# Half of the second group's first layer by twenty products, with its sums and a pair of halves put elsewhere in the order

## The chip, the cores and the metric
The kernel runs on one core of one Trainium2 chip. The metric is the device time of one execution in microseconds (us); smaller is better. The core has five engines with queues of their own: TensorE (PE, matmul), VectorE (DVE), ScalarE (ACT), GpSimd (POOL) and SyncE (SP, which here issues DMAs).

## What is computed
The reference is a recurrent attention followed by a two-layer network, all in float32:

```
for t in range(S):                     # S = 768, head_dim = 48, batch 4, 8 heads
    state = alpha[t] * state + k[t] (outer) v[t]
    y[t]  = q[t] @ state
x = y as (3072 tokens, 384)
h = x @ w_in                           # 384 x 2048
g = h * sigmoid(h)                     # silu
out = g @ w_out                        # 2048 x 384
```

The change concerns h = x @ w_in for a part of the tokens, and the order in which sums of weights, sums of tokens and sums of g are made.

## The kernel before, in words
**Tokens.** The 3072 tokens are 24 chunks of 128 (a chunk is 128 time steps of one of the four batches). Attention works chunk by chunk (`scores`, `products`, `quotient`, `values`, `states`, `flip`, `land`): DVE makes two scans, three transposes and some multiplies for each, PE the small matmuls, and `values` (L831) leaves the transposed output of two chunks in a tile `xt`. Four chunks make a group (six groups, `grp` 0 to 5); a group has two halves of two chunks, 256 tokens (`h` 0 and 1).

**First layer.** The 2048 columns of w_in are two pairs of quarters (`pair` 0 and 1), eight blocks of 128 columns each. There are two ways to make h for them:

- `enter_plain(grp, h, pair)` (L897) takes one half of the tokens and makes the eight column blocks in four pieces of two blocks, each block three matmuls of 128x256; ACT applies silu from PSUM to the tile of g (L909). Behind the fourth piece of groups above 0 stands `side_by_side` (L1016), which adds two cells of g on DVE (L1019).
- `enter(grp, pair)` (L917) takes both halves of the tokens at once and makes the same columns by 20 products instead of 24 (a 4x3 by 3x2 block product with fewer multiplications, listed in PRODUCTS, L349), each as two matmuls of 128x256. It needs 23 sums of blocks of w_in (SUMS_W, L335, made on DVE by `sums_w`, L589; some overwrite w_in, the others fill a tile `wx`), 11 sums of tokens (SUMS_X, L343, `sums_x`, L878, into `xc`), and puts the products together with 12 copies on ACT (L936, four of them into a tile `part` that has one buffer) and 14 additions on DVE (L944 and, for one, L587). It has seven steps, six of three products and one of two; the last step ends with `side_by_side` for both halves. Accumulators are three PSUM banks that take turns (`bank`, L894): a product that begins a new bank waits until the addition or copy that reads the old content is done.

Groups 0 and 1 use the plain way, groups 2 to 5 the other.

**Second layer.** `leave(grp, h)` (L1021) makes the output of a half by seven products of eight matmuls 128x192 each, with six subtractions of g on DVE (L1033), sums on DVE (L1074 to L1085) and stores (L1036 to L1045). It needs differences of w_out (`differences`, L600), which plain(1,0,0) makes.

**Order.** The list `pieces` (L1120 to L1136) holds generators of `enter_plain`, `enter`, `leave` and `sums_x` in their order; `fill` (L1166) runs as many of them after each slot of an attention step as the work done so far is behind an even pace, `phases` marking the places where the pace is set anew. Each step has four slots. For the stretch in question the order of the kernel before is:

- phase 0 ends with plain(1,0,0) and the seven steps of leave(0,0);
- phase 1: four pieces plain(1,1,0); then leave(0,1) by turns with four pieces plain(1,0,1) and four pieces plain(1,1,1);
- phase 2: sums_x(2); leave(1,0) by turns with enter(2,0); leave(1,1) by turns with enter(2,1); and so on for the later groups.

The sums of w_in are issued from `done()` (L1050), which each step of `leave` calls: leave(0,1) makes those of pair 0, leave(1,0) those of pair 1, four a step. `late` is filled, and with it `wx` allocated, by `settle()` (L1154) after slot 3 of step 7; by the pacing, leave(0,0) has then made three of its seven steps.

**Queues.** From `settle` on PE's instructions stay in program order (`in_order`, L381). Sums of weights and of tokens, the conversion of weights and the range checks on alpha and the weights (L685) keep their order among each other on DVE; the other DVE instructions are placed by the compiler's scheduler, and the order so found is fixed at compile time. The steps of the prediction refer to L909, L944, L1019, L1033 and the lines of attention (L696 transposes, L722 and L752 scans, L758 multiply).

Of the kernel before, what the change touches and what calls it, by code (L numbers as in the profile page):

```python
# [355 lines left out]
def quotients(  # L356
# [22 lines left out]
    late = {}  # L379
# [25 lines left out]
    GB = 4  # L405
# [183 lines left out]
    def sums_w(pair, upto):  # L589

        r = slice(2 * pair, 2 * pair + 2)
        while sums_done[pair] < min(upto, len(SUMS_W)):
            to, sa, a, sb, b = SUMS_W[sums_done[pair]]
            tc.keep_in_program_order(
                combine(block_w(to)[:, r], sa, block_w(a)[:, r], sb, block_w(b)[:, r]))
            sums_done[pair] += 1

    sums_done = [0] * (NQ // 2)

    def differences(i):  # L600

        if i < HF // 2:
            i = slice(2 * i, 2 * i + 2)
            tc.keep_in_program_order(
                dve.tensor_tensor(t1[:, i], b12[:, i], b11[:, i], ALU.subtract))
            dve.tensor_tensor(t2[:, i], b22[:, i], t1[:, i], ALU.subtract)
            dve.tensor_tensor(t4[:, i], b21[:, i], t2[:, i], ALU.subtract)
        else:
            i -= HF // 2
            side_by_side(0, i % 2, i // 2)  # L610
            i = slice(2 * i, 2 * i + 2)
            dve.tensor_tensor(b12[:, i], b22[:, i], b12[:, i], ALU.subtract)
# [265 lines left out]
    def sums_x(grp):  # L878
        xcs[grp] = late["xc"].tile([128, len(SUMS_X), TB], F32, name="xc")
        for to, sa, a, sb, b in SUMS_X:  # L880
            tc.keep_in_program_order(
                combine(block_x(grp, to), sa, block_x(grp, a), sb, block_x(grp, b)))
        yield
# [4 lines left out]
    def g_tiles(grp, pair):  # L888
        for h in range(2):
            gts[grp, h, pair] = gpool.tile([128, 4, 2, TB], F32, name="g")  # L890
# [6 lines left out]
    def enter_plain(grp, h, pair):  # L897

        if h == 0:
            g_tiles(grp, pair)  # L900
        xt = xts[2 * grp + h]
        for f in range(8 * pair, 8 * pair + 8, 2):
            ps = bank(f // 2 % 3).rearrange("p (e n) -> p e n", e=2)
            for e in range(2):
                for t in range(NKT):
                    pe.matmul(ps[:, e, :], lhsT=w_in[:, t, (f + e) * 128 : (f + e + 1) * 128],
                              rhs=xt[:, t, :], start=(t == 0), stop=(t == NKT - 1))
            q, i = divmod(f, 4)
            act.activation(gts[grp, h, pair][:, i : i + 2, q % 2, :], ps, AF.Silu)  # L909
            if grp == 1 and pair == h == 0:  # L910
                differences(f // 2)
                differences(4 + f // 2)
            if grp > 0 and f % 8 == 6:
                side_by_side(grp, h, pair)
            yield

    def enter(grp, pair):  # L917
        g_tiles(grp, pair)
        halves = [gts[grp, h, pair] for h in range(2)]

        s = [halves[o % 2][:, o // 2] for o in range(8)]
        todo = iter(PRODUCTS)

        def new(i):
            return bank(i).rearrange("p (e n) -> p e n", e=2)

        def add(ps, first=False):
            w, x = next(todo)
            for e in range(2):
                pe.matmul(ps[:, e], lhsT=block_w(w)[:, 2 * pair + e], rhs=block_x(grp, x),  # L930
                          start=(first and e == 0), stop=(e == 1), skip_group_check=True)

        def copy(ps, to=None):
            if to is None:
                to = late["part"].tile([128, 2, TB], F32, name="part")
            act.copy(to, ps)  # L936
            return to

        def silu(h, i):
            x = halves[h][:, i : i + 2]  # L940
            act.activation(x, x, AF.Silu)  # L941

        def tt(to, a, b, op=ALU.add):
            dve.tensor_tensor(to, a, b, op)  # L944

        a, b, c = [new(i) for i in range(3)]
        add(a, True)
        copy(a, s[6])
        add(b, True)
        copy(b, s[2])  # L950
        add(c, True)
        tt(s[6], s[6], copy(c), ALU.subtract)
        yield
        add(a)
        t = copy(a)
        add(b)
        copy(b, s[4])
        add(c)
        copy(c, s[7])
        tt(s[7], s[7], t, ALU.subtract)  # L960
        yield
        add(a)
        copy(a, s[5])
        add(b)
        copy(b, s[3])
        tt(s[5], s[5], s[3])
        add(c)
        copy(c, s[0])
        yield
        add(a)  # L970
        tt(s[4], a, s[4])
        b = new(1)
        add(b, True)
        add(b)
        copy(b, s[1])
        yield
        c = new(2)
        add(c, True)
        tt(s[2], s[2], copy(c), ALU.subtract)
        a = new(0)  # L980
        add(a, True)
        tt(s[6], a, s[6])
        silu(0, 2)
        add(b)
        tt(s[5], copy(b), s[5], ALU.subtract)
        yield
        add(c)
        tt(s[1], c, s[1])
        tt(s[3], s[1], s[3], ALU.subtract)
        a = new(0)  # L990
        add(a, True)
        tt(s[2], a, s[2])
        add(b)
        tt(s[7], b, s[7])
        silu(1, 2)
        yield
        add(c)
        combine(s[1], -1, s[1], -1, s[0])
        tt(s[0], c, s[0])
        silu(0, 0)  # L1000
        a = new(0)
        add(a, True)
        tt(s[3], a, s[3])
        silu(1, 0)
        turn.append(turn.pop(0))
        for h in range(2):
            side_by_side(grp, h, pair)
        yield
# [7 lines left out]
    def side_by_side(grp, h, pair):  # L1016

        x = cells(grp, h, pair, 1, 0)
        dve.tensor_tensor(x, x, cells(grp, h, pair, 1, 1), ALU.add)  # L1019

    def leave(grp, h):  # L1021
# [26 lines left out]
        steps = iter(range(7))  # L1048

        def done():  # L1050
            if 2 * grp + h in (1, 2):
                sums_w(2 * grp + h - 1, 4 * next(steps) + 4)

        def new(i):
            return out_bank(i, HO)
# [51 lines left out]
    def plain(grp, h, pair):  # L1107
        return (enter_plain(grp, h, pair), 12, 2 * (2 * grp + h) + 2)

    def group(grp):  # L1110
        return [[(enter(grp, pair), 12, GB * grp + GB)] * 7 for pair in range(2)]

    def output(grp):
        return [[(leave(grp, h), 12, GB * grp + GB)] * 7 for h in range(2)]
# [1 line left out]
    def both(x, y):  # L1116
        for i in range(max(len(x), len(y))):
            pieces.extend(x[i : i + 1] + y[i : i + 1])

    pieces = []  # L1120
# [3 lines left out]
    pieces += [plain(1, 0, 0)] * 4 + [(leave(0, 0), 12, GB)] * 7  # L1124
    phases = [len(pieces)]
    pieces += [plain(1, 1, 0)] * 4
    both([(leave(0, 1), 12, GB)] * 7, [plain(1, 0, 1)] * 4 + [plain(1, 1, 1)] * 4)
    phases.append(len(pieces))
    before = output(1)
    for grp in range(2, NG):  # L1130
# [10 lines left out]
    def go_on():  # L1141

        nonlocal done
        next(pieces[done][0], None)
        done += 1

    audits = audit()
    done, bridged = 0, 0
    STEPS = NT + 1
    SLOTS = 4  # L1150
# [148 lines left out]
```

## Time and profile before
| | us |
|---|---|
| median of 3 runs | 560.08 |
| lowest, highest run | 558.29, 560.13 |
| span of the profiled execution, first to last instruction | 558.1 |
| PE, DVE, ACT, POOL busy in it | 541.4, 445.1, 208.4, 75.9 |

Of the profiled execution only its span is known; what lies around it shows in the runs, the fastest of which is 0.2 us longer than the span. In the groups of the profile a name such as `ps_m<-xt,w_in` gives the output and inputs of an instruction; a float32 matmul of the source appears as two records. `ps_m` are the banks of the first layer, `ps_o` of the second, `ps_a` of attention. In a timeline the columns are start, duration, engine, line, operation and, in brackets, the idle time of the engine before it and what ended it.

### The profile page before, as it was taken

The page shows a single profiled execution, that of the slowest core. Times are in us where ns is not written, and L with a number is a line of the kernel's source. Part 1 is how long each engine was busy: PE and PEld are TensorE (multiplying, and loading weights), DVE is VectorE, ACT ScalarE, POOL GpSimd, SP SyncE. Part 2 cuts the span into 40 slices and gives each one's busy share as a digit, 9 for nine tenths or more (in the row PEclk, how much of TensorE's full clock was granted, in tenths as well). Part 3 has the DMA queues.
Part 4 walks back from the last instruction along what each step waited for, and adds up shares of the span by engine and source line. Part 5 has one row for each costly group of instructions (what it writes and reads, how often), then busy time and mean ns, then how long its engine had stood idle before and what let it go on. Part 6 is the DMA issues. An engine that isn't in the chain of part 4 may idle for free. (4 is left out here: it accounts for less than half of the span.)

```text
span 558.1 us, 12640 instructions
## 1 busy us (share of the span) xinstructions
PE 541.4 (97%) x5026; PEld 488.8 (88%) x5026; DVE 445.1 (80%) x801; ACT 208.4 (37%) x466; POOL 75.9 (14%) x146
## 2 busy tenths in 40 slices
PE   5999999999999999999999999999999999999996
PEld 3788887998899898899999999988998999998996
DVE  5887889974999799997998986998894775857531
ACT  3456643223333243353353353353263341432200
POOL 4100010221211211021021021021121000001000
PEclk9799999999999999999999999999999999999999
DMA  9999861164445525355445654717712122333101
GB/s 218 255 276 177 232 189 40 38 164 108 126 131 136 142 62 134 88 145 157 129 109 142 194 141 115 198 22 179 180 48 84 53 99 95 111 109 106 38 25 32
DMA packets 99220, 70.13 MB, mean 126 GB/s; under 512 B 56272, under 2 KB 88656, under 8 KB 99152
## 3 DMA queue, kind: packets, MB, share of 16 engines
q1 hardware_dynamic: 97232, 65.30, 44.6%
q0 software_dynamic: 1920, 3.93, 2.0%
q8 instruction: 41, 0.67, 0.5%
q14 instruction: 27, 0.22, 0.1%
HBM read 61.34 MB, written 7.86 MB: 124 GB/s over the span
## 5 line engine op out<-in xcount | busy, mean ns | idle before, releaser
L388 PE MATMUL ps_o<-w_out,g 128*128 128x192 f32 x768 | 134.7, 329 | 1.1 <-DVE o L1042 0.9
L388 PEld LDWEIGHTS ps_o<-w_out,g 128*128 128x128 f32 x768 | 125.4, 190 | 5.1 <-DVE o L1042 2.3
L388 PE MATMUL ps_m<-xt,w_in 128*128 128x256 f32 x480 | 113.6, 383 | 1.5 <-ACT xt L851 1.1
L388 PEld LDWEIGHTS ps_m<-xt,w_in 128*128 128x128 f32 x480 | 89.1, 190 | 14.4 <-ACT xt L851 1.6
L388 PE MATMUL ps_o<-wt,g 128*128 128x192 f32 x576 | 99.7, 326 | 0.0
L388 PEld LDWEIGHTS ps_o<-wt,g 128*128 128x128 f32 x576 | 95.1, 190 | 1.6 <-issue 0.2
L388 PE MATMUL ps_m<-xc,w_in 128*128 128x256 f32 x288 | 70.7, 382 | 0.0
L685 DVE TENSOR_REDUCE seen<-bits 128x1 f32<-128x384 int32 (+2 forms) x65 | 42.5, 689 | 24.0 <-DMA bits<-in_moe_w_out_dram 19.6
L388 PEld LDWEIGHTS ps_m<-xc,w_in 128*128 128x128 f32 x288 | 53.6, 190 | 7.0 <-DVE g L944 0.3
L941 ACT ACTIVATE g<-g 128x1024 f32<-128x1024 f32 x32 | 33.0, 1056 | 59.0 <-DVE g L944 59.0
L1033 DVE TENSOR_TENSOR g<-g 128x512 f32<-128x512 f32 x72 | 49.8, 708 | 6.1 <-PE ps_o L388 6.1
L1045 POOL DMA_DIRECT2D out_dram<-o x40 | 22.0, 550 | 223.2 <-DVE o L1042 127.6
L813 POOL TENSOR_SCALAR_AFFINE_SELECT g<-g 64x256 f32<-64x256 f32 x64 | 34.2, 534 | 124.8 <-ACT g L806 105.8
L388 PE MATMUL ps_m<-xc,wx 128*128 128x256 f32 x192 | 50.0, 383 | 1.0 <-DVE xc L586 1.0
L936 ACT COPY g<-ps_m 128x512 f32<-128x512 f32 x64 | 36.5, 588 | 36.5 <-PE ps_m L388 36.4
L388 PEld LDWEIGHTS ps_m<-xc,wx 128*128 128x128 f32 x192 | 35.2, 190 | 5.3 <-ACT u L1064 1.3
L944 DVE TENSOR_TENSOR g<-ps_m,g 128x512 f32<-128x512 f32 x56 | 37.0, 684 | 2.9 <-PE ps_m L388 2.7
L722 DVE TENSOR_TENSOR_SCAN u<-al,one 128x516 f32<-128x516 f32 x24 | 30.0, 1249 | 10.6 <-ACT al L719 10.3
L909 ACT ACTIVATE g<-ps_m 128x512 f32<-128x512 f32 x32 | 19.1, 596 | 42.8 <-PE ps_m L388 42.3
L936 ACT COPY part<-ps_m 128x512 f32<-128x512 f32 x32 | 18.9, 589 | 43.0 <-DVE g L944 21.3
L752 DVE TENSOR_TENSOR_SCAN p<-al,inv 128x516 f32<-128x516 f32 x24 | 29.9, 1246 | 1.0 <-PE ps_a L388 0.4
L388 PE MATMUL ps_a<-g,vn 128*32 128x128 f32 x768 | 27.5, 278 | 1.8 <-POOL g L801 1.7
(126 smaller groups left out, 611.4 us busy)
## 6 DMA issues: line engine op xcount, KB each, us to landing
bits<-in_moe_w_in_dram SPq DMA_DIRECT2D x24, 512.0 KB, 4.8
bits<-in_moe_w_out_dram SPq DMA_DIRECT2D x32, 384.0 KB, 3.1
at<-in_alpha_dram SPq DMA_DIRECT2D x64, 96.0 KB, 2.5
kt<-in_k_dram SPq DMA_DIRECT2D x64, 96.0 KB, 2.5
qt<-in_q_dram SPq DMA_DIRECT2D x64, 96.0 KB, 2.6
bits<-in_alpha_dram SPq DMA_DIRECT2D x9, 512.0 KB, 3.8
out_dram<-o POOLq DMA_DIRECT2D x40, 96.0 KB, 2.4
flips<-turn SPq DMA_DIRECT2D x12, 256.0 KB, 2.4
```

Of the source, the lines that this page charges most:

```text
L388: in_order(nc.tensor.matmul(*args, **kw))
L685: dve.tensor_reduce(seen[kind][which][:, i : i + 1], x, axis=AX, op=op, apply_absolute_value=True))
L722: dve.tensor_tensor_scan(u[:, end - 1 :: -1], sg[:, end:0:-1], one[:, end:0:-1], 0.0, ALU.mult, ALU.add)
L752: dve.tensor_tensor_scan(p[:, 0:end], sg[:, 0:end], iv[:, 0:end], 0.0, ALU.mult, ALU.add)
L813: gps.affine_select(x, x, pattern=[[0, NP], [1, CH]], compare_op=ALU.is_ge, fill=0.0, base=0, channel_multiplier=-1)
L909: act.activation(gts[grp, h, pair][:, i : i + 2, q % 2, :], ps, AF.Silu)
L936: act.copy(to, ps)
L941: act.activation(x, x, AF.Silu)
L944: dve.tensor_tensor(to, a, b, op)
L1033: dve.tensor_tensor(cells(grp, h, pair, *to), cells(grp, h, pair, *x), cells(grp, h, pair, *y), ALU.subtract)
L1045: (gps if grp < NG - 1 else nc.sync).dma_start(out[r : r + C, c * HO : (c + 1) * HO], o)
```

## The change
Pair 1 of group 1 is made by `enter(1, 1)` instead of plain(1,0,1) and plain(1,1,1), after a `sums_x(1)`. The sums of w_in for pair 1 are issued earlier: three after each step of leave(0,0) that runs once `late` is filled, four with each piece of plain(1,1,0), and what is left at the start of `enter`. The sums for pair 0 are issued later, in leave(1,0) instead of leave(0,1). Group 2 makes pair 1 first and pair 0 second. `side_by_side` after a plain half is issued one piece later: it is put on a list `owed` and issued after the next piece of `pieces`.

```
@@ enter_plain, enter @@
+            if grp == h == 1:
+                sums_w(1, sums_done[1] + 4)
             if grp > 0 and f % 8 == 6:
-                side_by_side(grp, h, pair)
+                owed.append((done, grp, h, pair))
             yield
 
     def enter(grp, pair):
+        sums_w(pair, len(SUMS_W))
         g_tiles(grp, pair)
@@ leave @@
         def done():
-            if 2 * grp + h in (1, 2):
-                sums_w(2 * grp + h - 1, 4 * next(steps) + 4)
+            if grp == h == 0 and late:
+                sums_w(1, sums_done[1] + 3)
+            if grp == 1 and h == 0:
+                sums_w(0, 4 * next(steps) + 4)
@@ the list of pieces @@
+    def second(grp, pair):
+        return [(enter(grp, pair), 12, GB * grp + GB)] * 7
+
     def group(grp):
-        return [[(enter(grp, pair), 12, GB * grp + GB)] * 7 for pair in range(2)]
+        return [second(grp, pair) for pair in ((1, 0) if grp == 2 else (0, 1))]
...
     pieces += [plain(1, 1, 0)] * 4
-    both([(leave(0, 1), 12, GB)] * 7, [plain(1, 0, 1)] * 4 + [plain(1, 1, 1)] * 4)
+    pieces.append((sums_x(1), 0, 2 * GB))
+    both([(leave(0, 1), 12, GB)] * 7, second(1, 1))
@@ go_on @@
         next(pieces[done][0], None)
+        while owed and owed[0][0] < done:
+            side_by_side(*owed.pop(0)[1:])
         done += 1
```

More of the change, by code (lines that the diff above doesn't have):

```diff
@@ L1144, in go_on @@
         next(pieces[done][0], None)
+        while owed and owed[0][0] < done:
+            side_by_side(*owed.pop(0)[1:])
         done += 1
     audits = audit()
+    owed = []
     done, bridged = 0, 0
```

## The prediction, made before the result was known
> **What bounds the kernel now.** I read the page's first part, then the busy time by stretch of work, then the waits of two engines, then the timeline where a wait is long. The page:
>
> ```profile
> PE 541.4 (97%) x5026; PEld 488.8 (88%) x5026; DVE 445.1 (80%) x801; ACT 208.4 (37%) x466; POOL 75.9 (14%) x146
> ```
>
> TensorE (PE) looks like the bound, VectorE (DVE) like the second engine, with ACT and POOL far off. But 80% is a mean over stages. The stretches below are cut where the order of work changes: the last leave(0,0), the four plain pieces of (1,1,0), then leave(0,1) with the plain halves of pair 1, then the first and the second half of group 2, then two halves of group 3. Columns: stretch, its length, then busy us (xinstructions) of each engine.
>
> ```profile
> 101.90:126.90 25.00, 24.77 (x310) 23.18 (x308) 20.36 (x36) 4.53 (x12) 6.34 (x11) 1.00 0.44 116
> 126.90:140.50 13.60, 13.57 (x168) 11.64 (x168) 5.79 (x9) 5.12 (x15) 1.64 (x4) 1.00 0.34 89
> 140.50:189.70 49.20, 48.72 (x578) 44.22 (x569) 44.98 (x81) 14.88 (x45) 9.17 (x16) 1.00 0.53 142
> 189.70:233.80 44.10, 42.75 (x441) 38.38 (x433) 43.36 (x87) 15.45 (x39) 6.21 (x12) 1.00 0.36 96
> 275.70:317.70 42.00, 42.00 (x442) 38.53 (x432) 40.09 (x69) 17.89 (x43) 6.08 (x12) 1.00 0.55 150
> ```
>
> The reader is to see two things. A half group takes 42.00 us where PE never stops (last row), but 44.10 in the fourth row, where DVE is busy for 43.36 of 44.10: there DVE, not PE, sets the pace. And in the second row DVE has 7.8 us to spare. The waits of DVE (96 to 230 us) and of PE (126 to 260 us) say why:
>
> ```profile
> DVE g L1019 <- ACT g L909: 10.1, 2, 7.6
> DVE al L696 <- DMA at<-in_alpha_dram: 1.5, 1, 1.5
> ...
> PE ps_m L388 <- DVE g L944: 1.3, 2, 0.9
> PE ps_a L388 <- DVE p L758: 0.5, 1, 0.5
> ```
>
> DVE stood still for 7.6 us on one side_by_side (L1019) that waits for the last silu of a plain half; 2.5 us more on a second one. PE stopped three times for DVE. The timelines of both engines show the places:
>
> ```profile
> 130.39 1.23 DVE L752 TENSOR_TENSOR_SCAN p<-al,inv 128x516 f32<-128x516 f32 x1
> 139.25 0.69 DVE L1019 TENSOR_TENSOR g<-g 128x512 f32<-128x512 f32 x1 [7.62 <-ACT g L909]
> ...
> 143.87 0.90 PE L388 MATMUL ps_a<-p,kp 48*64 48x128 f32 x32 [0.48 <-DVE p L758]
> ...
> 218.62 0.69 DVE L944 TENSOR_TENSOR g<-ps_m,g 128x512 f32<-128x512 f32 x1
> ...
> 219.37 1.13 PE L388 MATMUL ps_m<-xt,wx 128*128 128x256 f32 x4 [0.92 <-DVE g L944]
> ```
>
> At 219.37 PE wants the PSUM bank that DVE reads only at 218.62, though all products of that piece had ended by 213.9, where the next scores begin: the wait is the length of DVE's queue. It happens again at 230.72 (0.41 us).
>
> [...] The trace agrees (684 to 708 at L944 and L1033, about 420 at L582); but back to back the starts lie only 0.60 us (269.40, two at once, then 270.60) and 0.34 to 0.45 us apart, and a full queue is priced by these. [...] this is what 131.6 to 139.25 shows, where the transposes and scans behind the side_by_side lie idle with it. [...] I therefore take PE's price from the distance of pieces and not from the 383 ns of a matmul.
>
> **The change, part by part.**
> (1) Fewer products. A plain piece is six matmuls of 128x256 (twelve records: the trace has 1024 on ps_m for 512 in the source). In the timeline of ACT the silus of plain pieces that follow each other start at 133.44, 136.03 and 138.62, so a piece is 2.59 us of PE. Pair 1 of group 1 took eight pieces, 20.7 us. enter(1,1) has 20 products of two matmuls, 6 2/3 pieces of the same shape, 17.3 us. PE saves **3.45 us**.
> (2) What this costs DVE. enter has 14 additions of 128x512 (L944, L587) where a plain half has none: 14 x 0.60 = 8.4 us. sums_x(1) adds 11 of 128x256 at about 0.42 (the eleven of sums_x(2) go from 190.39 to 196.53 with 1.35 us of others between): 4.6 us. Together **13.0 us**. side_by_side keeps its four for group 1, two issued inside enter. ACT gains 12 copies of 0.59 and 4 silus of 1.06 for 8 of 0.60, 6.5 us more, in a stretch where it has 34 us free: nothing, unless its copies to "part" wait for DVE, which is DVE's delay once more.
> (3) Sums of w_in moved, none added. Pair 1's 23 leave group 2's first half for leave(0,0) (12, since the flag that allows them is set only after its third step: four steps of three) and plain(1,1,0) (11). Pair 0's 23 move from leave(0,1) into the place that pair 1's had. At 0.36 us each a set is 8.3 us. So the fourth row's DVE load stays as it is, and the swap of halves in group 2 is free: same products, same tiles, and the pair that goes first has its sums.
> (4) side_by_side a piece later. For (1,1,0) it now stands behind sums_x(1). The 7.6 us hole gets work in front of it: 11 sums of w_in (4.0), the rest of that chunk's attention (transposes, multiplies: 139.86 to 143.7, 3.8), sums_x (4.6). All are ready by then: the weights were last read in group 0, the tokens of chunk 7 are copied at 126.4. So PE's 0.48 us at 143.87 goes as well.
> No DMA is added; no queue of SP or POOL has anything moved past it but with its whole step. New waits: enter's additions wait for PE and ACT at the head of DVE's queue, with the next chunk's scans behind; leave(1,0) and enter(2,1) wait for enter(1,1)'s last additions as every later group does.
>
> **The sum.** On PE alone: 3.45 + 0.48 = 3.9 us, or 5.3 if the waits at 219.37 and 230.72 (0.92 + 0.41) went too. But between 140 and 252 us DVE has no reserve; PE can't be earlier at 219 than DVE's queue. DVE's idle gaps in front of that point, from the timeline, are 0.47, 0.61, 1.49, 0.23, 0.89 and 0.35 (110 to 127), 7.62, 0.41 and 2.49 us: 14.57 in all. Into them go 13.0 us of new work. If all is filled, DVE comes to the pinch 14.57 - 13.0 = 1.6 us earlier. I take off 0.3 for dependent additions that follow each other with gaps of 0.03 to 0.10 (as at 119.24): **1.3 us**, the gain, since after the pinch the stretches of 42.0 us run at PE's pace and can't win more. If none of the 4.04 us before 127 is filled (in them DVE waits for PE and DMA and the order may leave sums behind), it is 10.5 - 13.0 = -2.5, a loss. The unknown lies between, near the upper end, for the 1.49 us gap and its neighbours lie where the first sums become free.
> The span is 558.1 us, 0.2 below the fastest run (558.29); the median is 560.08. I subtract from the median: 560.08 - 1.3 = **558.8**.
>
> **Rivals.**
> A (my forecast): DVE's queue in group 2's first half caps the gain; 558.3 to 562.6. For: 43.36 of 44.10, and two PE waits on L944. Chance 0.50.
> B: the cap isn't felt, because the additions that free a bank come earlier in the queue than now (the one at 218.62 stands behind a transpose, a scan and four sums). Then PE's 3.9 to 5.3 us count: 556.2 to 554.8, say 556.1. For: the later halves run at 42.00 us with DVE at 40.09. Against: they have no sums of w_in. Chance 0.27.
> C, slower: the hole at 131.6 is not filled. [...] if another instruction that waits for PE or ACT takes the head there, or the sums are queued behind it, only 14.57 - 7.62 = 6.95 us of gaps remain for 13.0 us: DVE comes 6.1 us later to the pinch at 219 and PE waits for all of it: 566.2. It decides from the point where less than 10.2 us is filled (13.0 less 2.8, that is 0.5%): 562.9 to 566.2. For: this order put one such wait there already. Chance 0.23.
> That the change does nothing is excluded: eight matmuls are no longer issued.
>
> **How the numbers follow.** 0.5% is 2.8 us, about what a measurement of this kernel can tell from no change. B lies beyond it (0.26 of its 0.27), A within, C beyond on the other side (0.22 of 0.23): faster 0.26, same 0.52, slower 0.22. The range goes from 555.4, which leaves out the lower third of B (0.08), to 563.6, which leaves out most of C (0.12 or more with what is unforeseen). A's own range is 558.3 to 562.6.
>
> **What would show it.** (1) MATMUL records on ps_m fall from 1024 to 1008. (2) L944 and L587 on g have 14 more instructions, sums on xc 11 more. (4) No DVE wait over 3 us between 127 and 140, and no L758 wait of PE near 143. The cap: in group 2's first half PE still waits for DVE at L944, by 1 to 5 us in all. I am wrong if that stretch comes down to 42 us with PE never idle (B), or if DVE again stands over 5 us at one place before 190 (C).

## The result and the profile after

The changed kernel is slower: 562.71 us (median of 4 runs, 562.12 to 562.84), where the kernel before has 559.84 (median of 4 runs). The ratio is 1.0052, 95% interval 1.0037 to 1.0068. The prediction was 558.8, faster by 1.3 us; the loss is 2.9 us. The profiled execution has a span of 561.1 us, 3.0 more than before, in a run of 562.84 us: about 1.7 us lie around a span, not the 0.2 that the prediction took.

The page of the changed kernel: TensorE has the 16 records fewer that the 20 products promise (5026 to 5010), VectorE 25 instructions and 10 us more.

```profile
PE 541.1 (96%) x5010; PEld 487.0 (87%) x5010; DVE 455.1 (81%) x826; ACT 214.5 (38%) x474; POOL 77.1 (14%) x146
```

The busy time by stretch of the changed kernel, cut at the same events as before, to 0.1 us (columns: stretch, length, then busy us and instructions of PE, PEld, DVE, ACT, POOL, then clock, DMA share and GB/s):

```profile
102.39:127.37 24.98, 24.72 (x311) 23.22 (x309) 22.04 (x43) 4.53 (x12) 5.22 (x9) 1.00 0.38 100
127.37:140.97 13.60, 13.60 (x169) 11.66 (x169) 10.82 (x22) 5.22 (x15) 3.94 (x7) 1.00 0.45 119
140.97:188.92 47.95, 45.47 (x553) 41.05 (x553) 45.50 (x81) 18.33 (x50) 9.54 (x16) 1.00 0.48 129
188.92:235.22 46.30, 43.47 (x441) 38.54 (x433) 45.73 (x92) 17.77 (x41) 6.08 (x12) 1.00 0.40 109
277.47:319.41 41.94, 41.94 (x433) 38.58 (x433) 39.67 (x68) 17.58 (x42) 6.10 (x12) 1.00 0.56 151
```

The third row is the one in which the 20 products lie. PE's busy time falls by 3.2 us there (48.72 to 45.47), its length by only 1.2 (49.20 to 47.95). The fourth row, where no product was taken away, grows from 44.10 to 46.30 with DVE busy for 45.73 of it, in five instructions more (x87 to x92). So what the third row saves the fourth gives back, and more. The last row is as before: the later halves are untouched.

The waits of DVE between 96 and 236 us and those of PE in the whole changed kernel say where it stands still now:

```profile
DVE g L1022 <- ACT g L909: 2.6, 1, 2.6
DVE o L1045 <- PE ps_o L388: 1.4, 1, 1.4
DVE al L696 <- DMA at<-in_alpha_dram: 1.4, 1, 1.4
DVE g L1036 <- PE ps_o L388: 1.1, 2, 0.6
```

```profile
PE ps_a L388 <- DVE p L758: 2.5, 2, 1.3
PE ps_o L388 <- DVE o L1045: 2.1, 3, 1.2
PE ps_m L388 <- DVE xc L586: 2.0, 2, 1.0
PE ps_m L388 <- DVE g L947: 1.5, 2, 1.0
```

(L1022 is the addition of side_by_side, L947 the additions of enter, L1036 the subtractions and L1045 the stores of leave.) DVE's hole at the addition of side_by_side has shrunk from 7.6 to 2.6 us, but it has not gone; and PE waits for DVE in more places: for p 2.5 us where it was 0.5, for xc 2.0 (1.0 before), for the stores 2.1 (0.9 before). The timelines of DVE and of PE show the hole, the first of the two waits for p (the second, 1.34 us, comes at 162.52) and the pinch, which is the place where the prediction has PE wait at 219.37 for a bank that DVE has yet to read:

```profile
135.76 1.23 DVE L752 TENSOR_TENSOR_SCAN p<-al,inv 128x516 f32<-128x516 f32 x1
139.62 0.69 DVE L1022 TENSOR_TENSOR g<-g 128x512 f32<-128x512 f32 x1 [2.63 <-ACT g L909]
140.23 1.13 DVE L696 STREAM_TRANSPOSE turn<-kt 128x512 f32<-128x512 f32 x1
...
144.09 0.67 DVE L758 TENSOR_TENSOR p<-turn,p 128x512 f32<-128x512 f32 x1
144.68 1.08 DVE L582 TENSOR_TENSOR xc<-xt 128x256 f32<-128x256 f32 x3
...
220.04 0.69 DVE L947 TENSOR_TENSOR g<-ps_m,g 128x512 f32<-128x512 f32 x1
```

```profile
144.90 0.90 PE L388 MATMUL ps_a<-p,kp 48*64 48x128 f32 x32 [1.14 <-DVE p L758]
...
220.79 1.13 PE L388 MATMUL ps_m<-xt,wx 128*128 128x256 f32 x4 [1.05 <-DVE g L947]
```

The code issues the addition of side_by_side behind sums_x(1). In the queue it stands ahead of sums_x(1) (144.68) and ahead of the transpose of k (140.23), where it stood before the change: deferring it in the code did not move it, for the scheduler places it. The hole is smaller because 20 of the 23 sums of w_in run ahead of it.

**The sum on DVE.** From the start of leave(0,0) to the addition that frees the bank at the pinch (218.62 before, 220.04 after), I add the durations of DVE's records, the idle gaps over 0.1 us, and subtract what records overlap (one begins before the last has ended), where gaps under 0.1 us count against the overlap. These come to the length but for 0.1 us. "Net" is durations less overlap.

| kernel | length | instructions | durations | overlap | net | gaps |
|---|---|---|---|---|---|---|
| before | 116.70 | 179 | 107.50 | 5.90 | 101.6 | 14.99 |
| changed | 117.65 | 204 | 121.36 | 10.52 | 110.8 | 6.70 |

25 instructions add 13.9 us of durations, but only 9.2 us to the queue, because they overlap with their neighbours; and 8.3 us of gaps are filled, not 14.6. 9.2 less 8.3: DVE comes to the pinch 0.95 us later, and PE with it.

**The rest.** Positions below are those of products of leave in the trace, measured in each execution from the start of leave(0,0) (101.93 before), less the same for the kernel before, so that differences at the start of an execution drop out. The changed kernel is at +0.96 at the start of leave(1,1) and at +2.54 at the start of the last product (550.73 before). So a further 1.6 us is lost behind 234 us, where the prediction saw nothing to win or lose: 0.3 by the start of leave(2,0), 0.6 just before leave(4,1) (479.24 before) and 0.7 before leave(5,0) (515.68).

### The profile page after: what moved, and what is told of

It reads as the page before. It is cut to its first block, busy times and chain, and to the rows that moved or that the text cites. A ratio compares the mean times of both kernels' runs of the same rounds, so it can differ in the third digit from the quotient of the medians.

```text
span 561.1 us, 12640 instructions
## 1 busy us (share of the span) xinstructions
PE 541.1 (96%) x5010; PEld 487.0 (87%) x5010; DVE 455.1 (81%) x826; ACT 214.5 (38%) x474; POOL 77.1 (14%) x146
## 5 line engine op out<-in xcount | busy, mean ns | idle before, releaser
L388 PE MATMUL ps_m<-xt,w_in 128*128 128x256 f32 x396 | 94.8, 383 | 1.5 <-ACT xt L851 1.1
L388 PEld LDWEIGHTS ps_m<-xt,w_in 128*128 128x128 f32 x396 | 73.4, 190 | 12.9 <-ACT xt L851 1.6
L388 PE MATMUL ps_m<-xc,w_in 128*128 128x256 f32 x324 | 79.7, 382 | 0.3 <-DVE xc L582 0.3
L388 PEld LDWEIGHTS ps_m<-xc,w_in 128*128 128x128 f32 x324 | 60.3, 190 | 8.3 <-DVE xc L582 0.4
L685 DVE TENSOR_REDUCE seen<-bits 128x1 f32<-128x384 int32 (+2 forms) x65 | 42.6, 691 | 26.2 <-DMA bits<-in_moe_w_out_dram 21.7
L388 PE MATMUL ps_m<-xc,wx 128*128 128x256 f32 x216 | 56.3, 383 | 2.0 <-DVE xc L586 2.0
L939 ACT COPY g<-ps_m 128x512 f32<-128x512 f32 x72 | 41.0, 588 | 41.2 <-PE ps_m L388 41.1
L1036 DVE TENSOR_TENSOR g<-g 128x512 f32<-128x512 f32 x72 | 49.5, 704 | 6.3 <-PE ps_o L388 6.3
L388 PEld LDWEIGHTS ps_m<-xc,wx 128*128 128x128 f32 x216 | 39.6, 190 | 7.0 <-ACT u L1069 2.5
L947 DVE TENSOR_TENSOR g<-ps_m,g 128x512 f32<-128x512 f32 x63 | 41.7, 683 | 2.9 <-PE ps_m L388 2.7
L388 PEld LDWEIGHTS ps_a<-p,kp 48*64 48x64 f32 (+1 forms) x640 | 21.6, 151 | 9.8 <-issue 8.0
L388 PE MATMUL ps_a<-p,kp 48*64 48x64 f32 (+2 forms) x640 | 26.0, 264 | 2.6 <-DVE p L758 2.5
```

The lines of the kernel that those rows point to most:

```text
L388: in_order(nc.tensor.matmul(*args, **kw))
L685: dve.tensor_reduce(seen[kind][which][:, i : i + 1], x, axis=AX, op=op, apply_absolute_value=True))
L1036: dve.tensor_tensor(cells(grp, h, pair, *to), cells(grp, h, pair, *x), cells(grp, h, pair, *y), ALU.subtract)
```

## The experiments

All kernels of one group ran beside the kernel before on one chip; its medians were 559.1, 559.36, 560.57 and 559.03 us. Each group had another chip, so kernels of different groups are compared by their ratio to the kernel before or by positions in the trace, not by their medians. A ratio can differ by about 0.1% from the quotient of the two medians. Theory Q says that the loss comes from the addition of side_by_side, which still heads DVE's queue; L, that it comes from DVE's added work; T, that it comes from the range checks at the end (L685), behind which the stores of the last group wait. These three are not exclusive, so the runs had to give each its share. The fourth group is for what the first three leave open: which of DVE's instructions count, and whether the products are worth anything with everything else mended.

### First group: the queue's order, and the checks

**e1**: the changed kernel with the addition held where the code issues it.

```
-        dve.tensor_tensor(x, x, cells(grp, h, pair, 1, 1), ALU.add)
+        ins = dve.tensor_tensor(x, x, cells(grp, h, pair, 1, 1), ALU.add)
+        if pinned:
+            tc.keep_in_program_order(ins)
...
-            side_by_side(*owed.pop(0)[1:])
+            side_by_side(*owed.pop(0)[1:], pinned=True)
```

> The changed kernel, but the addition of g behind a plain half (side_by_side) is pinned in its new place, behind the instruction traced before it, so that for the half (1,1,0) it stands behind the eleven sums of tokens and no longer ahead of the next chunk's transposes. Theory Q (the addition still heads VectorE's queue and waits there for the last silu, 2.6 us idle, and all that is queued behind it comes late): the wait of 2.6 us at 139.6 goes, PE's waits for the next two scores (1.2 and 1.5 us) shrink to under 0.5 us each, time 559.5 to 561, that is 1.7 to 3 us under the changed kernel. Rival L (VectorE's load in the first half of group 2 sets the time, whatever happens before): the wait goes, but PE waits as much longer at the first-layer banks near 199 and 219, time 562.2 to 563. Rival T (the loss is in the tail, where range checks of the weights wait for DMA): 562 to 563, with the loss of 1.6 us after 277 us unchanged.

**e2**: the kernel before with the deferral alone, held in the same way, and none of the rest of the change.

> The kernel before with one part of the change alone: the addition of g behind a plain half is issued a piece later, and pinned there. Theory Q: the 7.6 us wait of VectorE before 139.25 goes or falls under 3 us, PE's 0.48 us wait at 143.9 goes, and since VectorE then comes earlier to the banks near 218 and 230, part of 1.3 us there too: 0.5 to 1.8 us faster than before. Rival L: the banks near 218 stay as late as they are, so only 0.5 us. Rival T: no change beyond 0.5 us.

**e3** and **e4**: the changed kernel and the kernel before without the range checks of w_in and w_out (those of alpha stay).

```
-        if wide:
+        if False:
             todo += [(moe_w_in[t * 128 : t * 128 + 128, c : c + 512], 512, 1)
...
```

> The changed kernel without the range checks of w_in and w_out (the 28 fetches and 56 reductions are left out, those of alpha stay). Rival T (1.6 of the 3.0 us are lost in the tail where these checks wait for DMA at the head of VectorE's queue): this kernel is only 1.0 to 1.7 us slower than the kernel before without the same checks. Theory Q: what the change costs arises before 236 us; the two differ by 1.0 us there, and the remaining 1.6 us must come from elsewhere, so the difference stays at 2.5 to 3 us. Both kernels without checks are faster than with them by 1 to 4 us.

> The kernel before without the range checks of w_in and w_out, as the partner of the changed kernel without them. Both theories: faster than before by 1 to 4 us, since PE's 0.9 us of waiting for a store in the tail goes and the last additions come earlier. The difference between the two is what tells: 1.0 to 1.7 us for rival T, 2.5 to 3 us for theory Q with a loss elsewhere.

| kernel | median us | ratio to before (95%) | at leave(1,1) | at the last product |
|---|---|---|---|---|
| e1 | 559.74 | 1.0012 (1.0001 to 1.0022) | -0.97 | +0.90 |
| e2 | 558.21 | 0.9979 (0.9971 to 0.9987) | -1.10 | -0.76 |
| e3 | 560.14 | 1.0022 (1.0014 to 1.0030) | +1.07 | -0.32 |
| e4 | 558.47 | 0.9991 (0.9983 to 0.9999) | +0.10 | -1.57 |

In e1 the hole is gone; the timeline of its DVE around the same place:

```profile
134.86 1.23 DVE L752 TENSOR_TENSOR_SCAN p<-al,inv 128x516 f32<-128x516 f32 x1
136.01 1.07 DVE L696 STREAM_TRANSPOSE turn<-kt 128x512 f32<-128x512 f32 x1
...
139.90 0.68 DVE L758 TENSOR_TENSOR p<-turn,p 128x512 f32<-128x512 f32 x1
```

The transpose follows the scan without an idle time, the multiply for p comes 4.2 us earlier than in the changed kernel (1.2 us of it because this execution's leave(0,0) is earlier), and the next scores no longer wait for it. The order of the queue is thus worth 1.9 us at leave(1,1) (+0.96 to -0.97) and 0.40% of the time, as theory Q has it. But e2, which has none of the 20 products, is as early there (-1.10) and gains 0.21% itself, so about half of the 0.40% is a gain that the kernel before can have too. With the queue in order in both, the 3.45 us that PE saves are worth nothing at leave(1,1): something else takes all of them, and the second group asks whether it is L. e3 against e4 has 1.7 us between the medians where the full kernels have 2.9: without the checks 1.2 us of the loss is absent, as theory T has it, though this difference is uncertain by about 1 us. The traces say the same: what is lost behind leave(1,1) falls from 1.6 us to 0.3 (e3 less e4), and the loss at leave(1,1) stays. By itself e4 gained 0.6 us, where its text expected 1 to 4.

### Second group: DVE's work

**e5**: e1, with six of pair 1's sums at the end of `settle`.

```
         load(NA)
+        sums_w(1, 6)
```

> The changed kernel with the one addition of side_by_side kept in program order behind sums_x(1), and six of pair 1's sums of w_in issued at the end of settle(), ahead of the transposes of chunk 8, so that these six run in the idle time of VectorE before 116 us. Theory Q/L (VectorE's work between 119 and 160 us is what TensorE waits for in the second group's first half): some 2 to 3 us of VectorE's work leave that stretch, the waits of TensorE for p, xc and g shrink, the start of leave(1,1) moves forward against the pinned kernel by 1 to 2 us, and the time is 0.2 to 0.4% under the kernel before (557 to 558.5 where before is 559.5). Rival: the stretch is bound by the wait for the k tile's DMA and by the xc blocks, which come behind sums_x(1) whatever stands ahead: start of leave(1,1) as in the pinned kernel to 0.3 us, time within 0.15% of before.

**e6**: the changed kernel without DVE's work for enter(1,1): its 14 additions and the 11 sums of tokens are left out of the computation; the products take plain blocks of x instead.

```
+        if grp == 1:
+            return block_x(1, at % (2 * NKT))
...
         def tt(to, a, b, op=ALU.add):
-            dve.tensor_tensor(to, a, b, op)
+            if grp > 1:
+                dve.tensor_tensor(to, a, b, op)
...
-        combine(s[1], -1, s[1], -1, s[0])
+        if grp > 1:
+            combine(s[1], -1, s[1], -1, s[0])
...
-    pieces.append((sums_x(1), 0, 2 * GB))
```

> The changed kernel without the 14 additions that make the products' outputs of enter(1,1) from its seven sums, without sums_x(1), and with plain blocks of x in place of the sums in those products: TensorE has the same 1008 records of ps_m, and VectorE is spared 25 additions, about 13 us of durations. These additions are left out of the computation. Theory Q/L (the saving of TensorE is eaten by VectorE's added work and by the order of its queue): most of the 3.45 us comes back, the start of leave(1,1) is 2.5 to 4 us earlier than in the kernel before against leave(0,0), and the time is 554.5 to 557.5 where before is 559.5 (ratio 0.991 to 0.996). Rival A (a transfer or ScalarE bounds that stage whatever VectorE does): no earlier than the pinned kernel, ratio 0.999 to 1.002. Rival T (the range checks of w_out at the end set the time): the start of leave(1,1) is early by 2.5 us or more, but the end is within 1 us of before.

**e7** and **e8**: the changed kernel and e5 with the checks begun earlier.

```
-        if at % 2 == 0 and step > 3 * GB + 2:
+        if at % 2 == 0 and step > 3 * GB + 0:
```

> The changed kernel with the range checks of alpha, w_in and w_out begun three steps earlier, one every second slot as before (six more lie inside the loop, and the chain of fetch and reduction behind the last step is shorter by about six times 4.07 us). Rival T (about 1.2 us of the loss is the last group's waits behind that chain): the wait of ps_o for o goes from 2.1 us to about 1, and the time falls by 0.8 to 1.5 us against the changed kernel (ratio to before 1.002 to 1.004 where the changed kernel has 1.005). If the checks cost what they cost wherever they stand, the ratio stays at 1.005 or rises.

> The edits of e5 and e7 together: addition of side_by_side in program order, six sums at settle(), checks begun three steps earlier. If the losses at the front and at the tail are separate, they add: e5's ratio less 0.002, about 0.994 to 0.996 (556 to 557.5 where before is 559.5), faster than both kernels. If they are one lateness seen twice, it is within 0.001 of e5.

(The edit moved the checks by two steps, and four of them into the loop, not by three and six as these two texts have it.)

| kernel | median us | ratio to before (95%) | at leave(1,1) | at the last product |
|---|---|---|---|---|
| e5 | 560.60 | 1.0023 (1.0015 to 1.0031) | -0.01 | +1.35 |
| e6 | 557.16 | 0.9962 (0.9947 to 0.9977) | -3.72 | -2.81 |
| e7 | 566.00 | 1.0116 (1.0100 to 1.0132) | +1.88 | +7.80 |
| e8 | 564.60 | 1.0101 (1.0084 to 1.0118) | +0.94 | +3.18 |

e6 decides for DVE's work: without it the whole saving of PE shows at leave(1,1), 3.7 us, and the ratio is 0.9% under the changed kernel's, at the edge of the 0.991 to 0.996 expected. The 3.7 us are the 3.45 of the prediction's step 1, plus the wait at the pinch, which is gone (0.92 before), less a longer wait for p (1.14 us, 0.48 before). Up to these 3.7 us no transfer and no other engine bounds that stage.

e5 missed (-0.01 at leave(1,1), where e1 has -0.97), on the other side from what theory L expected. Its DVE timeline shows why: in e1 DVE waits 1.65 us for the DMA of a chunk and then transposes alpha, 12.9 us behind the start of leave(0,0). In e5 all six sums stand ahead of that transpose, take 3.1 us, and it comes 14.3 us behind that start. The chain of transposes and scans of the chunk goes back with it; PE waits once for u, 1.4 us, a wait that e1 does not have:

```profile
PE ps_o L388 <- DVE u L1081: 1.4, 1, 1.4
```

e7 missed too. In the tail alone it did what T said: from leave(4,1) (479.24 before) to the last product it gains 1.0 us on the kernel before where the changed kernel loses 0.7. But with four checks moved into the stages before, it loses 7.0 us between leave(1,1) and leave(4,1) (+1.9 to +8.8), where the changed kernel loses 0.8 (+1.0 to +1.8). A check is not free in the loop; why four are so dear was not tried. e8, with the other front, missed in the same way: it loses 3.4 us on that stretch (+0.9 to +4.3), where its text expected a ratio of 0.994 to 0.996.

### Third group: the tail otherwise, and the sums of tokens

**e9**, **e10**, **e11**: behind the last step the loop issues 29 pieces between 17 checks in place of 26, in the changed kernel, in e1 and in e2. **e12**: the changed kernel without the 11 sums of sums_x(1) (left out of the computation), with the 14 additions.

```
-        for _ in range(1 + turns % 2):
+        for _ in range(2 if turns % 3 else 1):
             go_on()
```

> The changed kernel; behind the last step, between two range checks of w_out, the loop issues 2, 1, 2, 2, 1, 2... pieces (29 with 17 checks) where it issued 2, 1, 2, 1... (26). A fetch and its reduction follow one another in about 4.07 us and a piece of TensorE's work is 2.60 us: 1.5 pieces are 3.90 us, less than the 4.07, so TensorE runs up to the chain and waits (0.17 us for each check, about 2.9 us over 17 of them, less what the PSUM banks let it run ahead); 1.67 pieces are 4.34 us, more than 4.07. Rival T: the two stalls of TensorE at 479 and 515 us go, the time falls 1.5 to 2.5 us against the changed kernel, ratio to before 1.001 to 1.003. Otherwise (the stalls are where VectorE's stores stand whatever the distance): 1.004 to 1.006.

> The pinned kernel (e1) with the tail of e9. If front and tail add: ratio to before 0.996 to 0.999 (e1's 1.0012 less 1.5 to 2.5 us of 559.5), faster than both kernels. If the tail gives back what the front saves: as e1, 1.000 to 1.002.

> The kernel before with side_by_side deferred and kept in program order (e2, ratio 0.998) and the tail of e9. The kernel before has a chain 65.1 us long for 24 pieces (62.4 us), with 0.9 us of waits of TensorE in it, so the tail is worth 0.7 to 1.5 us here: ratio 0.995 to 0.997. If this is below e10, the products by 20 in the second group's second half are a loss even with the queue and the tail in order; if it is above e10, they are a gain that the queue's order and the tail hid.

> The changed kernel without sums_x(1), with plain blocks of x in place of the eleven sums in the products of enter(1,1); the eleven sums are left out of the computation, the fourteen additions are kept. e6, without both, was 4.6 us faster than the changed kernel at the start of leave(1,1) against leave(0,0). If VectorE's load counts by its durations, these eleven (4.6 of 13.0 us) are worth 35% of that, 1.6 us; if what counts is that sums_x(1) stands in the queue ahead of k's and q's transposes and the xc blocks are waited for (PE waits for xc 2.0 us), they are worth 2.5 us or more, and the time is 0.3 to 0.5% under the changed kernel.

| kernel | median us | ratio to before (95%) | at leave(1,1) | at the last product |
|---|---|---|---|---|
| e9 | 561.42 | 1.0018 (1.0009 to 1.0028) | +1.13 | +0.68 |
| e10 | 559.00 | 0.9968 (0.9954 to 0.9983) | -1.14 | -1.61 |
| e11 | 557.74 | 0.9949 (0.9933 to 0.9966) | -0.86 | -2.51 |
| e12 | 562.42 | 1.0033 (1.0022 to 1.0043) | +0.09 | +2.60 |

e9 and e10 came out as their texts have it, e11 just under its range. e12 fits neither of its two cases: it is 0.9 us earlier than the changed kernel at leave(1,1), and no clear part of the time is gained. The tail of the changed kernel, in the timelines of DVE and PE, is a store held up in DVE's queue by a reduction that had to wait for its DMA:

```profile
508.70 1.01 DVE L685 TENSOR_REDUCE seen<-bits 128x1 f32<-128x384 int32 x2 [2.80 <-DMA bits<-in_moe_w_out_dram]
...
512.66 1.01 DVE L685 TENSOR_REDUCE seen<-bits 128x1 f32<-128x384 int32 x2 [0.94 <-DMA bits<-in_moe_w_out_dram]
...
516.77 1.00 DVE L685 TENSOR_REDUCE seen<-bits 128x1 f32<-128x384 int32 x2
517.69 0.68 DVE L587 SCALAR_TENSOR_TENSOR g<-g 128x512 f32<-128x512 f32 x1
518.29 0.34 DVE L1045 TENSOR_TENSOR o<-ps_o,u 128x192 f32<-128x192 f32 x1
```

```profile
518.69 3.25 PE L388 MATMUL ps_o<-w_out,g 128*128 128x192 f32 x16 [1.25 <-DVE o L1045]
```

The reductions (pairs on one buffer) follow each other at 4.1 us in the mean (3.9 to 4.6 from 475 to 521 us), and 1.5 pieces of PE's 2.60 us are 3.9: PE runs up to the chain and waits. With 1.7 pieces for a check it hardly does. The waits of PE for the stores, first in the kernel before, then in e9, where the changed kernel has 2.1 us:

```profile
PE ps_o L388 <- DVE o L1042: 0.9, 2, 0.7
```

```profile
PE ps_o L388 <- DVE o L1045: 0.3, 1, 0.3
```

So the looser tail is worth 0.34% to the changed kernel (1.0052 to 1.0018), 0.44% to e1 and 0.30% to e2, each uncertain by 0.1 to 0.2%: it helps the kernel before nearly as much. Front and tail add: 0.52 less 0.40 (e1) less 0.34 (e9) is -0.22%, and e10, with both, has -0.32%, intervals of 0.15 each way. Part of the gain is lost again at the very end: in e9 to e11 the span ends 5.3 to 5.4 us behind DVE's last addition, where before and the changed kernel have 4.1.

### Fourth group: which of the work, the swap, and the products with all mended

**e13**: the changed kernel without the 14 additions alone (left out of the computation), e6's edit without what concerns the sums of tokens. **e14**: the changed kernel with group 2's halves in their old order.

```
-        return [second(grp, pair) for pair in ((1, 0) if grp == 2 else (0, 1))]
+        return [second(grp, pair) for pair in (0, 1)]
```

**e15** and **e16**: e11 and e10 with 3 and 3 pieces in place of 5 and 4 around the last product of the checks.

> The changed kernel without the fourteen additions of enter(1,1) (they are left out of the computation); the eleven sums of sums_x(1) are kept. e6, without both, was 4.6 us earlier at the start of leave(1,1) against leave(0,0) than the changed kernel, e12, without the eleven sums, 0.9 us. If the shares add, the fourteen additions are worth 3.7 us there and the ratio to before is 0.997 to 0.999; if each set hides behind the other (either one alone leaves VectorE late), they are worth 1 to 2 us and the ratio is 1.001 to 1.004.

> The changed kernel with the third group's halves in the order of before, (2,0) ahead of (2,1). Then enter(2,0) needs all 23 sums of pair 0 at its first piece and issues them at once, 23 times 0.34 to 0.45 us, about 8.5 us, at the start of the stage behind 190 us, and pair 1's sums are in place 40 us before they are needed again. If the swap is what makes the late sums free (step 3 of the prediction), this is slower than the changed kernel by 3 to 8 us (ratio 1.010 to 1.020), and leave(1,1) starts that much later. If the slack of VectorE there takes the sums in any order, it is within 0.5 us of the changed kernel.

> e11 (the kernel before, addition of side_by_side deferred and kept in program order, more pieces between the range checks) with 3 and 3 pieces in place of 5 and 4 around the last product of the checks, so that six pieces stay behind the read of the result, as in the kernel before, and not three. In e9, e10 and e11 the span ended 5.3 to 5.4 us behind the last addition, where before and the changed kernel have 4.1. If that is the branch behind the read, which comes too near the end, the gap goes back to 4.1 and the time falls 1.2 us under e11 (ratio 0.992 to 0.994); if it is the last stores, it stays, ratio 0.994 to 0.996.

> e10 (the changed kernel, pinned, more pieces between the range checks) with the same end as e15. In its profile e10 stood at leave(2,0) against leave(0,0) where e11 stood, to 0.03 us: the saving of 3.45 us by the 20 products and the cost of the 25 additions of VectorE there cancel. So this is within 0.6 us of e15. If the products by 20 still cost something that the profiles of e10 and e11 do not show, it is over 1 us slower than e15; if they gain, it is faster.

| kernel | median us | ratio to before (95%) | at leave(1,1) | at the last product |
|---|---|---|---|---|
| e13 | 556.62 | 0.9955 (0.9939 to 0.9970) | -3.74 | -1.95 |
| e14 | 567.54 | 1.0140 (1.0123 to 1.0157) | +5.33 | +8.29 |
| e15 | 557.59 | 0.9968 (0.9955 to 0.9981) | -0.90 | -2.60 |
| e16 | 558.59 | 0.9989 (0.9982 to 0.9995) | -0.81 | -1.17 |

e13 reaches e6 at leave(1,1) to 0.02 us, with the 11 sums still in. The shares do not add as its text supposed: left out alone, the additions are worth 4.7 us there and the sums 0.9, both together 4.7. The table of DVE's sum, continued with the kernels that matter, shows how:

| kernel | length | durations | overlap | net | gaps |
|---|---|---|---|---|---|
| e1 (pinned) | 115.72 | 122.09 | 10.83 | 111.3 | 4.34 |
| e2 (before, pinned) | 115.60 | 107.83 | 5.86 | 102.0 | 13.52 |
| e12 (without 11 sums) | 116.78 | 117.80 | 10.42 | 107.4 | 9.29 |
| e13 (without 14 additions) | 112.95 | 112.47 | 7.71 | 104.8 | 8.08 |
| e6 (without both) | 112.96 | 108.05 | 6.75 | 101.3 | 11.56 |

From e6 to e13 the 11 sums add 3.5 us of net work and take 3.5 us of gaps: length the same. From e13 to the changed kernel the 14 additions add 6.1 us and find 1.4 us of gaps: 4.7 us longer. In the other order, from e6 by way of e12, the additions cost 3.8 us and the sums 0.9. Either way the additions are most of the cost. They also read the banks of enter(1,1), so that e13 frees these sooner; but in the changed kernel PE waits for no addition before 189 us (its waits for L947 lie at 220.79 and 232.15), so the time was not lost there. The stretch of the products and the one behind it show where it was; first e13, then the first of them in the changed kernel (the second is the fourth row above), then e1 (columns as above, cut at the starts of leave(0,1), leave(1,0) and leave(1,1)):

```profile
139.20:185.58 46.38, 45.24 (x560) 41.17 (x552) 42.40 (x74) 20.69 (x53) 10.60 (x16) 1.00 0.54 144
185.58:228.82 43.24, 42.74 (x440) 38.37 (x432) 42.50 (x86) 15.55 (x39) 7.12 (x12) 1.00 0.39 106
```

```profile
140.90:188.92 48.02, 45.54 (x561) 41.12 (x553) 45.57 (x81) 18.40 (x50) 9.54 (x16) 1.00 0.48 129
```

```profile
139.98:185.81 45.83, 45.47 (x561) 41.09 (x553) 43.45 (x76) 18.42 (x50) 9.74 (x16) 1.00 0.48 126
185.81:232.11 46.30, 43.47 (x440) 38.52 (x432) 45.73 (x92) 17.77 (x41) 6.10 (x12) 1.00 0.40 109
```

Of the 4.7 us that the additions cost the changed kernel, 1.64 lie in the stretch of the products (46.38 to 48.02) and 3.06 in the next (43.24 to 46.30). With the queue in order (e1, which differs from e13 in this as well) the first part is gone: that stretch is no longer than in e13 (45.83, PE at work for 45.47 of it), so PE has its saving there. The next one is as long as in the changed kernel, though none of the 14 additions was placed in it by the code: DVE carries a queue over, six instructions more than in e13 (x86 to x92), and is busy for 45.73 of 46.30. The saving is made in one stretch and given back in the next.

e14 shows what the swap is for: with the old order enter(2,0) needs pair 0's sums at once, and PE stands, in its timeline,

```profile
199.11 1.22 PE L388 MATMUL ps_m<-xc,wx 128*128 128x256 f32 x2 [4.64 <-DVE wx L586]
```

for 4.64 us. The swap is needed, and the sums of w_in are free only with it.

e16 is slower than e15 by 1.0 us between medians (0.9989 against 0.9968, with intervals that just do not meet; e10 against e11 gave the same 0.2%, with intervals that overlap), as the second half of its expectation has it. Of this the front accounts for 0.1 us at leave(1,1) and 0.4 at leave(2,0); at the last product it is 1.4. (A position comes from one execution; e1, e10 and e16, which have the same front, stand at -0.97, -1.14 and -0.81 at leave(1,1), so 0.3 us is within its scatter.) So with order and tail mended the 20 products still lose about 0.2%, most of it in the tail, and what makes the difference there was not settled. The later end of the span did not go back (5.3 us in e15), and e15's ratio lies above both of its ranges. It is not the number of pieces behind the read; e3 and e4, whose loop is as it was, end as late (5.3 and 5.4 us). What it is stays open.

The lowest ratio of a kernel that leaves nothing out is e11's, 0.9949: the kernel before with the deferral held in order and the looser tail. e15, with the same front, has 0.9968, and the two intervals overlap. Both make pair 1 of group 1 in the plain way.

## Why the prediction was wrong

**The base.** It put 0.2 us around the span; the runs have 1.7. This did not matter, since the gain was taken off the median.

**Step 1, fewer products: right.** 1008 records of ps_m were foretold (396 + 324 + 216 + 72 are there), and 3.45 us; e6 and e13 show 3.7 us at leave(1,1), which is 3.45 and the change of two waits.

**Step 2, DVE's work: right in kind, two sizes off.** DVE's queue does cap the gain, and L947 makes PE wait at the pinch, 1.5 us in all, within the 1 to 5 foretold. The durations were foretold as 13.0 at queue distances; the records add 13.9, of which 4.6 overlap, so the queue grows by 9.2. That error was in the kernel's favour. The reasoning also gave additions and sums one price. e12 and e13 show that they differ in what they cost PE: the sums go into gaps, most of the additions do not. By the order in which they are taken out, the additions cost 3.8 to 4.7 us and the sums 0 to 0.9.

**Step 3, the sums moved for nothing: right as a whole** (e14 shows what it rests on). That the fourth row's load of DVE would stay as it was is wrong: it went from 43.36 to 45.73, by what the third row had left over.

**Step 4, the step that failed.** "For (1,1,0) it now stands behind sums_x(1)": it does not. The change issues it there, and the scheduler put it back ahead of the transpose of k, so the hole was filled by 5 us, not 7.6; the multiply for p came later than before, and PE's 0.48 us became 1.14 instead of going, with a second such wait of 1.34 us behind it. The sign "no DVE wait over 3 us between 127 and 140" came out (2.63 us) by the sums that run ahead of the addition, not by its being moved. "If all is filled" counted 14.57 us of gaps; 8.3 were filled. Of the 6.7 left, 2.6 are the hole, 2.5 lie ahead of it (the gap of 1.49 us, near which the first sums were to be free, is still 1.37 us, for the first sum starts behind it, at 119.89) and 1.4 are a new wait of a store for PE (L1045). With 9.2 of work that gives +0.95 where -1.3 was foretold. Held in order (e1), 10.65 us are filled against 9.66 of work: 1.0 us earlier. That this is near the 1.3 of the sum is luck in part: the gaps filled and the work were each 3 to 4 us less than the sum has them, which cancels, and e2 with the deferral alone is as early, so none of that 1.0 us is owed to the 20 products. Rival B (the cap isn't felt) is out: only with the additions gone does leave(1,1) come 3.7 us earlier, near its 3.9, and even then 0.45% of the time is gained (e13), about 2.5 us. Rival C named the mechanism ("another instruction that waits for PE or ACT takes the head there"), and the head was taken by the very one that was to move. C's sum had less filling and dearer work than there was; its range of 562.9 to 566.2 begins just above the 562.71 measured.

**The part that was not there.** "After the pinch the stretches of 42.0 us run at PE's pace and can't win more": they can lose. 1.6 us more was lost from leave(1,1) to the last product, 1.3 of it from just before leave(4,1) on, where the stores stand in DVE's queue behind the checks; without the checks 1.2 us of the loss is absent (e3, e4), and a looser tail is worth 0.34% (1.9 us, e9). No step of the prediction looked at the tail, though the profile before has PE wait 0.9 us for the stores there.

The order of the queue is worth 0.40% to the changed kernel (e1) and the pace of the tail 0.34% (e9). Together that is more than the loss of 0.52%, since both mends also improve the kernel before: the deferral held in order by 0.21% (e2), and the tail on top of it by 0.30% (e11). To split the loss, compare like with like: 0.52% as the kernels are, 0.33% with the order held in both (e1, e2), 0.19% with the tail looser in both as well (e10, e11; e16 and e15 have 0.21%). So the order of the queue makes about 0.2 of the loss, the tail's pace 0.1, and 0.2 stays with the rest of the change, the products and their additions; each of these is uncertain by 0.1 to 0.2. That DVE's additions eat the products' saving is shown by e6 and e13; that nothing is left of it even when mended, by e16 against e15.

## What to carry to other kernels

Before exchanging matmuls for additions, see whether the additions' engine has idle time that the additions can reach: here the 14 additions brought 6.1 us of net work and found 1.4 us of gaps (e13 to the changed kernel). Look at the stretch, and at the next one, for a queue that is carried over shows its cost there: 3.06 of the 4.7 us here. Where a scheduler places instructions, moving one in the code may move nothing: the addition of side_by_side stayed ahead of the transpose of k, with 2.63 us of idle time before it, and only held in order (e1) did it leave that place. And when a time is off by half a per cent, look at the tail as well: here reductions 4.1 us apart stood ahead of the last stores in DVE's queue, and more work of PE between them was worth 0.34% to the changed kernel, 0.44% to e1 and 0.30% to e2.

## What was not expected of the hardware

Records of DVE overlap in these traces, so that their durations overstate what a full queue took: among independent ones, a sum of 128x256 that lasts 0.42 us is followed after 0.34 us by the next instruction (123.21, 123.55 in the changed kernel) and one of 128x512 that lasts 0.68 after 0.60 (223.92, 224.52), while a sum of 128x256 that needs the one before starts 0.45 behind it (119.89, 120.34). Adding 25 instructions of 13.9 us raised the overlap from 5.9 to 10.5 us: here work strewn among other work cost the queue two thirds of its durations.

Filling a gap cost more than leaving it: in e5 3.1 us of sums that were issued at a gap of 1.65 us sent the chain behind it 1.4 us back. Two of these six took 1.62 us together (113.40 to 115.02) where the same two take 0.42 and 0.43 in e1. They lie beside two selections on POOL, as the timeline of e5's POOL has them:

```profile
113.34 1.41 POOL L801 TENSOR_SCALAR_AFFINE_SELECT g<-g 128x512 f32<-128x512 f32 x2 [0.49 <-ACT g L800]
```

The pair of selections takes 1.41 us here and 1.21 us in the changed kernel (114.74), where DVE runs a transpose beside it and no sum. Whether the sums and the selections slow each other was not shown: no run here was made to test it.
